# A fused attention and gated-FFN block: the fifth FFN product at two levels in both token passes, with two weight sums on Pool

## The chip, the cores and the metric

The kernel runs on one core of a Trainium2 chip. TensorE (PE) multiplies, with a weight load (PEld) ahead of each matmul; VectorE (DVE), ScalarE (ACT) and GpSimd (POOL) do the elementwise work; SyncE (SP) issues nearly all DMAs. Each engine runs its own instructions in program order, and semaphores order the engines against each other. The metric is device microseconds (us) of one execution.

## The reference

For 2048 tokens of width D = 1024: layer norm, linear attention, a residual, layer norm, a gated FFN of width F = 3584, a second residual.

```python
h = x + A(layernorm(x))          # qkv, phi, linear attention, @ wo
y = layernorm(h)
gate = y @ W_gate;  gate = gate * (gate > 0)
up   = y @ W_up
out  = h + (gate * up) @ W_down
```

## The kernel before, in words

**Order.** The program plans every instruction with its readers and writers (`PL.add`) and derives the semaphores; the order on each engine is the order of the calls. After attention come the output product `a4_mm` with its residual `a4_h` (L1252), then two token passes of 1024 tokens. Each pass is 14 FFN units (`ffn_unit`) and a down projection (`down_pass`).

**A unit.** A unit makes two 128-column blocks of gate (even unit) or of up (odd unit), called u = 0 and 1, for 1024 tokens. It does so with seven products instead of eight (Strassen's scheme in Winograd's form): `P1`, `P6`, `P2`, `P5`, `P7`, `P3`, `P4`, each of four 128x512 matmuls per u. The sums that this needs are the token sums `Ssum` (tile RC, four per pass) and the weight sums `Tring` (tile RO): four per unit, `T1` to `T4`, made by `t_sums` (L1354) from the weights in RWG, each a subtraction of 128x1024 elements for both u at once. `T2` reads `T1`, and `T4` reads `T2`. `T1` is the weight side of `P5`, `T2` of `P6`, `T3` of `P7`, `T4` of `P4`. All four run on DVE, apart from those of the very first unit, which run on Pool in halves of 128x512.

**Two levels.** In pass 1 (`L2F = (1,)`) product 5 is itself split into seven smaller ones, `M1` to `M7`, of 2 matmuls of 128x256 each, where the plain form has 8 matmuls of 128x512. This takes inner token sums `xs5` (`x_inner`, four per pass), inner weight sums `g5` (`w_inner`, three instructions per unit, L1395), copies of partial results on ACT (`M1c`, `M6c`, `M7c`, `M4c`), and two additions `s5_add` on DVE (L1514). The copies and additions use one PSUM bank with `M4` and `M3`: on PE, `M4` waits until `s5_add(1)` has read that bank.

**Evacuation.** The results of `P7` and `P3` get product 5 added on DVE (`evac5`, L1456, PSUM plus a tile). An even unit then applies relu on ACT; an odd unit multiplies gate and up on DVE (L1462, and L1470 straight from PSUM).

**Work between the products.** `fill` is a list of DVE work for the next unit, of which `fillin(n)` takes n items at fixed places of the unit; `mid` holds lists that are run at other fixed places. In pass 0 these bring in the weight sums for the down projection (`wd_sums` L706, `wl_sums` L729 on DVE and L745 on Pool, with their stores), sums of finished activations (`hh_sums`, L1366 and L1369), and the late layer norm of tokens 1024 to 2047 (ACT squares and means, small Pool steps, ACT norm). The Pool sums of `wl_sums` wait for the PE instruction just planned. At the end of a unit SP issues weight loads for a unit three later.

A pair of units in pass 0 (even, odd) is the period of this schedule.

Of the kernel before, what the change touches and what calls it, by code (L numbers as in the profile page):

```python
# [6 lines left out]
ALU = mybir.AluOpType  # L7
# [125 lines left out]
def bass_sequential_preLN__linear_attn_block__glu_gated_reglu__prompt_kernel(  # L133
# [15 lines left out]
    _, S, D = A_x.shape  # L149
# [7 lines left out]
    NW = 512  # L157
# [48 lines left out]
    with es:  # L206
# [70 lines left out]
        ftmp = RE[:, 0:(NO + NOT) * D].bitcast(f32).rearrange("p (a b) -> p a b", b=SBW)  # L277
        c22 = RE[:, 2 * D:3 * D].rearrange("p (a b) -> p a b", b=SBW)
        c12 = RE[:, 3 * D:4 * D].rearrange("p (a b) -> p a b", b=SBW)
        xs5 = RE[:, 4 * D:6 * D].bitcast(f16).rearrange("p (j k t) -> p j k t", j=4, k=2)  # L280
        g5 = RE[:, 6 * D:8 * D].bitcast(f16).rearrange("p (s j c) -> p s j c", s=2, j=4)
        hnE = RE[:, 4 * D:8 * D].rearrange("p (t a c) -> p t a c", t=STB, c=P)
        o0 = (NO + NOT) * D
        x2r = RE[:, o0:o0 + NX2 * D].rearrange("p (a b) -> p a b", a=NX2)
# [49 lines left out]

        hres = RX[:, 0:NHR * NW].rearrange("p (a b) -> p a b", a=NHR)
        outst = RX[:, 2 * NHR * NW:(2 * NHR + NOS) * NW].rearrange("p (a b) -> p a b", a=NOS)
        lsum = RX[:, 0:16 * HNW].bitcast(f16).rearrange("p (o j c) -> p o j c", o=4, j=4)
        dsf = RX[:, 0:STB * 2 * SBW].bitcast(f32).rearrange("p (a b) -> p a b", a=STB)
        zeros_t = hsb[:, 0, 0:512]
# [130 lines left out]
        def flat(x):  # L470
            return [b for row in x for b in (flat(row) if isinstance(row, list) else [row])]
# [38 lines left out]
            b_.over = B_E + B_bt + [B_TWq[2], B_junk]  # L510
        for b_ in B_hres + B_ds:
            b_.over = B_lsum
        for b_ in B_outst:
            b_.over = B_E + B_bt + [B_TWq[2], B_junk]
        for b_ in B_hnE:
            b_.over = B_o + B_oT
        for b_ in B_V:
            b_.over = B_hnE
        for b_ in flat(B_hh) + B_out2:
            b_.over = flat(B_xnT) + flat(B_pqT)  # L520
        for b_ in flat(B_pqT):
            b_.over = flat(B_wkv)
# [814 lines left out]
                lambda: add(3, blk(1, 0), Ssum[:, 1], ALU.subtract, [B_S[1]] + bl(0)),  # L1337
            ]

        def t_sums(L, eng="dve"):  # L1340
            i = L % NWG
            k = L % NTR
            n = 1 if eng == "pool" else 2

            def wb(kk, h, u):
                return wring[:, i + u:i + u + n, kk * KH:(kk + 1) * KH, h * P:(h + 1) * P]

            def tb(j, u):
                return Tring[:, k + u:k + u + n, j]

            def add(j, f0, f1, td):
                def go(u):
                    r = range(u, u + n)
                    PL.add(eng, lambda e: e.tensor_tensor(out=tb(j, u), in0=f0(u), in1=f1(u), op=ALU.subtract),  # L1354
                           reads=[B_w[i + x] for x in r] + ([B_T[k + x][td] for x in r] if td is not None else []),
                           writes=[B_T[k + x][j] for x in r], name="T%d_%d" % (j + 1, L))
                return [lambda u=u: go(u) for u in range(0, 2, n)]

            return (add(0, lambda u: wb(0, 1, u), lambda u: wb(0, 0, u), None) +
                    add(1, lambda u: wb(1, 1, u), lambda u: tb(0, u), 0) +  # L1360
                    add(2, lambda u: wb(1, 1, u), lambda u: wb(0, 1, u), None) +
                    add(3, lambda u: wb(1, 0, u), lambda u: tb(1, u), 1))
# [7 lines left out]
                                                    in1=hh[:, f1, SBW:2 * SBW], op=ALU.subtract),  # L1370
                   reads=[B_hh[f1][0]], writes=[B_hh[f1][1]], name="D3_%d" % q)

        def x_inner():
# [12 lines left out]
        def w_inner(n):  # L1386
            z = n % 2
            k = (2 * n) % NTR
            bt = [B_T[k][0], B_T[k + 1][0]]

            def T(kh, u):
                return Tring[:, k + u, 0, 2 * kh:2 * kh + 2, :].rearrange("p a c -> p (a c)")

            def add(dst, a_, b_, rd, wr):
                PL.add("dve", lambda e: e.tensor_tensor(out=dst, in0=a_, in1=b_, op=ALU.subtract), reads=bt + rd,  # L1395
                       writes=wr, name="g5_%d" % n)
# [10 lines left out]
        def ffn_unit(ps_, n, fill, mid):  # L1407
# [3 lines left out]
            kt = [(Lg + u) % NTR for u in range(2)]  # L1411
            f0 = 2 * (n - up)
            BA, BE, BB, BC_ = [0, 1], [2, 3], [4, 5], [6, 7]
            if ps_ in L2F:
                BE, BB = BB, BE
            if up:
                BB, BC_ = BC_, BB
# [65 lines left out]
            def p2(u):  # L1483
                prod(u, BA[u], w_blk(u, 1, 0), a_blk(1, 0), False, "P2")
                evac(0, 0, u, BA[u], "h11")

            if ps_ in L2F:
                cX, cD, c0 = ps[:, BE[1], 0:SHB], ps[:, BE[1], SHB:2 * SHB], ps[:, BE[0], 0:SHB]
                B_X = B_D = B_bank[BE[1]]
                tb = [B_T[kt[0]][0], B_T[kt[1]][0]]  # L1490
# [5 lines left out]

                def B_(kh, u):
                    return (lambda kk: Tring[:, kt[u], 0, 2 * kh + kk, :]), [tb[u]]

                def G(j):  # L1500
                    return (lambda kk: g5[:, z, j, kk * P:(kk + 1) * P]), [B_g5[z][j]]
# [24 lines left out]
                s5(1, 0, cX, B_X, "M6c")  # L1526
                sub(c0, B_bank[BE[0]], B_(1, 0), A(0, 1), False, "M2")
                fillin(2 if up else 3)
                p2(0)
                go(mid[2])  # L1530
                sub(cX, B_X, G(2), XS(2), False, "M7")
                s5(1, 1, cX, B_X, "M7c")
                s5_add(1)
                p6(0)
                p2(1)
                p6(1)
# [6 lines left out]
                       writes=[B_X, B_s5[0]], name="M4c")  # L1543
                go(later)
                later.clear()
                fillin(2 if up else 3)
                s5_add(0)
                B_s5[1].over = B_s5q[1]
# [523 lines left out]
        flush()  # L2072
        LAG = NOT
        pool_t = t_sums(0, "pool")
        for t in range(NE, NST + LAG + 1):
            if LAG <= t < NST + LAG:
                a4_mm(t - LAG)
            if t < NST:
                a2_num(t)
                a2_div(t)  # L2080
            if LAG <= t < NST + LAG:
                a4_h(t - LAG)
            if LAG + 1 <= t < TPP + LAG + 1:
                a4_norm(t - LAG - 1)
            if t in (5, 7, 18, 19):
                load_w_next()
            if t >= 9:
                run(pool_t, 1)
            if 15 <= t < 19:
                s_sums()[t - 15]()  # L2090
        load_w_next()
        load_w_next()
        for q in range(NWR):
            load_wraw(q)
        wl_q = []
        L2F = (1,)
        ln_q = []
        LQ = 3

        for p_ in range(NPASS):  # L2100
            fill = []
            for q in range(NPAIR):
                if q + 1 < NPAIR:
                    t_ = t_sums((p_ * NPAIR + q + 1) * 2)
                    if p_ in L2F:
                        t_ = t_[0:1] + w_inner(q + 1) + t_[1:]
                    fill = fill + t_
                mid = [[], [], [], [], []]
                if q > 0 and q % 2 == 0:
                    mid[0].append(lambda q=q: hh_sums(q - 2))  # L2110
                    mid[3].append(lambda q=q: hh_sums(q - 1))
                if p_ == 0:
# [8 lines left out]
                        ln_q.append(n_)  # L2121
                    if 2 <= q - LQ < 2 + STB:
                        early_t(q - LQ - 2)
                    mid[0] += wl_q
                    wl_q.clear()
                    if q % 2 == 0:
                        mid[1].append(lambda: wd_sums(q))
                    else:
                        w0_, w1_, mid[4] = wl_sums(q // 2)
                        mid[0].append(lambda: wd_sums(q))  # L2130
                        if q < NPAIR - 1:
                            mid[1].append(w0_)
                            wl_q.append(w1_)
                        else:
                            mid[0] = [load_wd_next] * 2 + mid[0] + [w0_, w1_]
                else:
                    if q == 0:
                        claim(B_xr + flat(B_lx), B_wd[0:NWS - 3])
# [24 lines left out]
            assert not fill  # L2163
            hh_sums(NPAIR - 2)
            hh_sums(NPAIR - 1)
            if p_ in L2F:
                claim(B_V, B_xs5 + flat(B_g5))
            late = []
            if p_ + 1 < NPASS:
# [13 lines left out]
                if p_ + 1 in L2F:  # L2183
                    def claim_xs():
                        claim(B_xs5, B_V)
                        claim(flat(B_g5), B_V)

                    gi = w_inner(0)
                    xi = x_inner()
# [62 lines left out]
```

## Time and profile before

| | us |
|---|---|
| median of 3 runs | 725.68 (725.53 to 727.32) |
| the profiled execution, its own time | 725.28 |
| its span | 723.5 |
| pass 0, 14 units | 229.75 to 398.96 |
| down projection of pass 0 | 398.96 to 476.76 |
| pass 1, 14 units | 476.76 to 643.20 |
| down projection of pass 1 | 643.20 to the end |

| stretch | length | PE busy | DVE busy | ACT busy | POOL busy |
|---|---|---|---|---|---|
| pass 0, units | 169.21 | 169.21 | 144.38 | 109.32 | 40.14 |
| pass 1, units | 166.44 | 166.44 | 134.10 | 83.53 | 3.54 |

Busy time is the time in which at least one instruction of the engine is in flight; back-to-back instructions overlap by some tens of ns, so that busy time is less than count times mean. A row of a timeline gives start, duration, engine, source line, operation, tiles (out<-in), shapes and count, and in brackets the idle time before it with what ended it. The source line of a helper is shared by all its callers: L767 is every matmul, L772 every plain ACT copy, L1661 the down projection's additions.

### The profile page before, as it was taken

What the parts mean: (1) busy time and instruction counts of PE and PEld (TensorE: products, weight loads), DVE (VectorE), ACT (ScalarE), POOL (GpSimd) and SP (SyncE); (2) the same over time, 40 slices, a digit from 0 to 9 for tenths busy, and PEclk for the clock granted to TensorE, in tenths of its full rate; (3) what the DMA queues carried; (4) which work ended last, traced back from release to release, by engine and by line L of the source; (5) the groups of instructions that cost most, each with busy time, mean ns of one, the idle gap of its engine ahead of it and who ended that gap; (6) DMA issues with size and microseconds to landing.
All of it is one profiled execution on the core that took longest, in us unless ns stands there. A gap on an engine that the chain in (4) does not pass through costs nothing.

```text
span 723.5 us, 12104 instructions
## 1 busy us (share of the span) xinstructions
PE 717.1 (99%) x4521; PEld 384.6 (53%) x4521; DVE 587.2 (81%) x1024; ACT 361.0 (50%) x632; POOL 109.5 (15%) x177
## 2 busy tenths in 40 slices
PE   9999999999999999999999999999999999999998
PEld 4444444344444444444444568865555555547887
DVE  7878867799776889888988787787889877887984
ACT  4878666764841456687757111035455545423010
POOL 1411100000360103322321002310000000000331
PEclk9999999999999999999999999999999999999999
DMA  9652244023998897999999999994555572037996
GB/s 316 207 115 61 37 131 156 13 29 68 195 229 258 245 267 228 281 296 264 326 298 276 302 265 315 320 211 119 149 166 140 158 248 81 1 102 252 315 321 174
DMA packets 192986, 143.59 MB, mean 198 GB/s; under 512 B 51872, under 2 KB 170400, under 8 KB 192928
## 3 DMA queue, kind: packets, MB, share of 16 engines
q1 hardware_dynamic: 188224, 138.50, 66.6%
q0 software_dynamic: 4032, 3.67, 3.6%
q8 instruction: 35, 0.57, 0.3%
q10 hardware_dynamic: 672, 0.66, 0.3%
q14 instruction: 23, 0.19, 0.1%
HBM read 98.76 MB, written 32.51 MB: 181 GB/s over the span
## 4 chain that ended last, share of the span: by engine, by line
PE 89%; DVE 6%; ACT 2%; issue 1%; SPq 1%; DMA 1%; POOL 0%; DVEq 0%; ACTq 0%
PE ps L767 89%; SPq L565 1%; DVE RAB L853 1%; DMA RE<-in_A_x_dram 1%; DVE RE L1228 1%; DVE RX L850 1%; ACT RX L846 1%; DVE RX L1069 1%; ACT RXH L805 1%; DVE RW L963 0%; DVE RWG L988 0%; ACT ps L772 0%; DVE RE L853 0%; DVE rden L1226 0%; DVE RE L1661 0%
## 5 line engine op out<-in xcount | busy, mean ns | idle before, releaser
L772 ACT ACTIVATE ps<-ps 128x512 f32<-128x512 f32 (+1 forms) x192 | 108.8, 567 | 218.0 <-PE ps L767 210.8
L767 PE MATMUL ps<-RC,RO 128*128 128x512 f16 x616 | 143.0, 369 | 0.0
L767 PE MATMUL ps<-RH,RWG 128*128 128x512 bf16 x448 | 108.1, 379 | 0.0
L767 PEld LDWEIGHTS ps<-RC,RO 128*128 128x128 f16 x616 | 60.3, 98 | 63.5
L767 PE MATMUL ps<-RC,RWG 128*128 128x512 f16 x320 | 76.8, 380 | 0.1
L767 PEld LDWEIGHTS ps<-RH,RWG 128*128 128x128 bf16 x448 | 43.8, 98 | 46.9
L767 PE MATMUL ps<-RH,RO 128*128 128x512 bf16 (+1 forms) x256 | 61.2, 379 | 0.0
L1470 DVE TENSOR_TENSOR RAB<-ps,RAB 128x512 bf16<-128x512 f32 x56 | 37.3, 686 | 29.4 <-PE ps L767 29.3
L767 PE MATMUL ps<-RW,RE 128*128 128x512 bf16 x256 | 57.6, 380 | 0.7 <-DVE RXH L1252 0.7
L1670 POOL DMA_DIRECT2D out_dram<-RX x20 | 17.9, 1256 | 263.3 <-DVE RX L1661 221.0
L767 PE MATMUL ps<-RAB 128*128 128x512 bf16 (+2 forms) x270 | 57.1, 351 | 0.1
L767 PE MATMUL ps<-RW,RAB 128*128 128x256 f16 (+3 forms) x362 | 52.9, 301 | 0.0
L767 PEld LDWEIGHTS ps<-RC,RWG 128*128 128x128 bf16 (+1 forms) x320 | 30.0, 98 | 40.0 <-ACT ps L772 6.0
L772 ACT ACTIVATE RE<-ps 128x512 f32<-128x512 f32 (+1 forms) x64 | 31.5, 503 | 37.8 <-PE ps L767 37.8
L767 PEld LDWEIGHTS ps<-RW,RAB 128*128 128x128 f16 (+1 forms) x362 | 35.4, 98 | 14.4 <-DVE RX L1661 0.2
L1354 DVE TENSOR_TENSOR RO<-RWG 128x1024 f16<-128x1024 bf16 x54 | 37.0, 684 | 6.4 <-DMA RWG<-in_B_W_up_dram 4.7
L1661 DVE TENSOR_TENSOR RE<-ps,RE 128x512 f32<-128x512 f32 x44 | 30.2, 687 | 14.3 <-PE ps L767 13.8
L772 ACT ACTIVATE RAB<-ps 128x512 bf16<-128x512 f32 x56 | 33.3, 594 | 16.6 <-PE ps L767 16.3
L767 PEld LDWEIGHTS ps<-RH,RO 128*128 128x128 f16 (+1 forms) x256 | 24.4, 98 | 30.0 <-ACT RX L772 1.6
L1456 DVE TENSOR_TENSOR RAB<-ps,RE 128x512 bf16<-128x512 f32 x56 | 37.1, 685 | 2.8 <-PE ps L767 1.9
L767 PEld LDWEIGHTS ps<-RW,RE 128*128 128x128 bf16 x256 | 24.0, 98 | 28.7 <-DVE RXH L1252 1.2
L1465 ACT ACTIVATE RAB<-RAB 128x1024 bf16<-128x1024 bf16 x28 | 29.5, 1055 | 19.4 <-DVE RAB L1456 18.9
(163 smaller groups left out, 1168.7 us busy)
## 6 DMA issues: line engine op xcount, KB each, us to landing
RWG<-in_B_W_gate_dram SPq DMA_DIRECT2D x28, 512.0 KB, 6.8
RWG<-in_B_W_up_dram SPq DMA_DIRECT2D x28, 512.0 KB, 5.5
RW<-l_scr SPq DMA_DIRECT2D x20, 448.0 KB, 5.8
RW<-in_B_W_down_dram SPq DMA_DIRECT2D x14, 512.0 KB, 5.7
t_scr<-RW SPq DMA_DIRECT2D x14, 512.0 KB, 5.0
l_scr<-RX SPq DMA_DIRECT2D x7, 1024.0 KB, 5.9
RE<-l_scr SPq DMA_DIRECT2D x15, 448.0 KB, 4.5
RE<-in_A_x_dram SPq DMA_DIRECT2D x23, 256.0 KB, 3.3
```

The lines of the kernel that those rows point to most:

```text
L565: return PL.add(eng, lambda e: e.dma_start(dst_ap, src_ap), reads=reads, writes=writes, slot=slot, name=name)
L767: lambda e: e.matmul(out_ap, lhsT, rhs, start=start, stop=stop, skip_group_check=skip),
L772: PL.add("act", lambda e: e.activation(out=dst, in_=src, func=func), reads=reads, writes=writes, name=name)
L805: PL.add("act", lambda e: e.activation(out=junk[:, c0:c1], in_=src[:, c0:c1], func=func, scale=scale, accum_out=sv[:, col:col + 1]), reads ...
L846: PL.add("act", lambda e: e.activation(out=Et[:, k, :], in_=src, func=ACTF.Exp), reads=[src_buf], writes=[B_E[k]], name=name + "_exp")
L850: PL.add("dve", lambda e: e.tensor_scalar(out=Et[:, k, :], in0=Et[:, k, :], scalar1=1.0, scalar2=1e-6, op0=ALU.min, op1=ALU.add), reads=[] ...
L1354: PL.add(eng, lambda e: e.tensor_tensor(out=tb(j, u), in0=f0(u), in1=f1(u), op=ALU.subtract), reads=[B_w[i + x] for x in r] + ([B_T[k + x] ...
L1456: PL.add("dve", lambda e: e.tensor_tensor(out=d, in0=src, in1=ftmp[:, u, :], op=ALU.add), reads=[bsrc, B_s5[u]], writes=[db], name=name)
L1465: PL.add("act", lambda e: e.activation(out=d, in_=d, func=ACTF.Relu), reads=[], writes=db, name=name)
L1470: PL.add("dve", lambda e: e.tensor_tensor(out=d, in0=bank(b), in1=d, op=ALU.mult), reads=[B_bank[b]], writes=[db], name=name)
L1661: PL.add(eng, lambda e: e.tensor_tensor(out=dst, in0=in0, in1=in1, op=op), reads=reads, writes=writes, name=name)
L1670: PL.add("pool", lambda e: e.dma_start(dst, src, accum_op=ALU.add), reads=[bsrc], writes=[B_hscr[st]], slot=sl, name="acc_%d_%d" % (st, dh))
```

## The change

- Product 5 goes at two levels in pass 0 too, apart from its first unit: `L2F = (0, 1)` and the condition `ps_ + n > 0`. The inner sums of pass 0 have their own places (`xs5s[0]` in RX, `g5s[0]` in RAB); the token ones are made at the end of attention (steps 16 and 17 of that loop), with `w_inner(0, 0)` at its last steps.
- In both passes `T3` and `T4` of the next unit go to Pool (`tail="pool"`), still 128x1024 each.
- The places of other work shift: in a two-level unit `mid[2]` runs after `M4c` and not before `M7`, `wl_sums`' second half runs in `mid[3]`, and the last unit of pass 0 spreads its `mid[0]` over `mid[5]`, `mid[6]` and `mid[0]`.

```diff
-        def t_sums(L, eng="dve"):
+        def t_sums(L, eng="dve", tail=None):
...
             def add(j, f0, f1, td):
+                en = tail if tail and j >= 2 else eng
+
                 def go(u):
                     r = range(u, u + n)
-                    PL.add(eng, lambda e: e.tensor_tensor(out=tb(j, u), in0=f0(u), in1=f1(u), op=ALU.subtract),
+                    PL.add(en, lambda e: e.tensor_tensor(out=tb(j, u), in0=f0(u), in1=f1(u), op=ALU.subtract),
...
-            if ps_ in L2F:
+            if ps_ == 1:
                 BE, BB = BB, BE
...
-            if ps_ in L2F:
+            if ps_ in L2F and ps_ + n > 0:
...
                 fillin(2 if up else 3)
+                go(mid[5])
                 p2(0)
-                go(mid[2])
                 sub(cX, B_X, G(2), XS(2), False, "M7")
                 s5(1, 1, cX, B_X, "M7c")
                 s5_add(1)
+                go(mid[6])
                 p6(0)
...
                 go(later)
                 later.clear()
+                go(mid[2])
                 fillin(2 if up else 3)
                 s5_add(0)
...
         pool_t = t_sums(0, "pool")
+        gi = w_inner(0, 0)
...
+            if t == 16:
+                for f_ in x_inner(0)[0:2]:
+                    f_()
+            if t == 17:
+                for f_ in x_inner(0)[2:4]:
+                    f_()
+            if t >= NST:
+                run(gi, 1)
...
-        L2F = (1,)
+        L2F = (0, 1)
...
-                    t_ = t_sums((p_ * NPAIR + q + 1) * 2)
+                    t_ = t_sums((p_ * NPAIR + q + 1) * 2, tail="pool")
                     if p_ in L2F:
-                        t_ = t_[0:1] + w_inner(q + 1) + t_[1:]
+                        t_ = t_[0:1] + w_inner(p_, q + 1) + t_[1:]
...
-                    mid[0] += wl_q
+                    mid[3] += wl_q
...
-                            mid[0] = [load_wd_next] * 2 + mid[0] + [w0_, w1_]
+                            mid[5] = [load_wd_next] * 2 + mid[0]
+                            mid[6], mid[0] = [w0_], [w1_]
```

More of the change, by code (lines that the diff above doesn't have):

```diff
@@ L279, in bass_sequential_preLN__linear_attn_block__glu_gated_reglu__prompt_kernel @@
         c12 = RE[:, 3 * D:4 * D].rearrange("p (a b) -> p a b", b=SBW)
-        xs5 = RE[:, 4 * D:6 * D].bitcast(f16).rearrange("p (j k t) -> p j k t", j=4, k=2)
-        g5 = RE[:, 6 * D:8 * D].bitcast(f16).rearrange("p (s j c) -> p s j c", s=2, j=4)
+        o5 = NFT * TOK
+        g5s = [x.bitcast(f16).rearrange("p (s j c) -> p s j c", s=2, j=4)
+               for x in (RAB[:, o5:o5 + 2 * D], RE[:, 6 * D:8 * D])]
         hnE = RE[:, 4 * D:8 * D].rearrange("p (t a c) -> p t a c", t=STB, c=P)
@@ L336, in bass_sequential_preLN__linear_attn_block__glu_gated_reglu__prompt_kernel @@
         outst = RX[:, 2 * NHR * NW:(2 * NHR + NOS) * NW].rearrange("p (a b) -> p a b", a=NOS)
+        xs5s = [x.bitcast(f16).rearrange("p (j k t) -> p j k t", j=4, k=2)
+                for x in (RX[:, 2 * NHR * NW:(2 * NHR + NOS) * NW], RE[:, 4 * D:6 * D])]
         lsum = RX[:, 0:16 * HNW].bitcast(f16).rearrange("p (o j c) -> p o j c", o=4, j=4)
@@ L512, in bass_sequential_preLN__linear_attn_block__glu_gated_reglu__prompt_kernel @@
             b_.over = B_lsum
-        for b_ in B_outst:
+        for b_ in B_xs5:
             b_.over = B_E + B_bt + [B_TWq[2], B_junk]
@@ L518, in bass_sequential_preLN__linear_attn_block__glu_gated_reglu__prompt_kernel @@
             b_.over = B_hnE
-        for b_ in flat(B_hh) + B_out2:
+        for b_ in flat(B_hh) + flat(B_g5):
             b_.over = flat(B_xnT) + flat(B_pqT)
@@ L1371, in hh_sums, with x_inner @@
                    reads=[B_hh[f1][0]], writes=[B_hh[f1][1]], name="D3_%d" % q)
-        def x_inner():
+        def x_inner(ps_):
+            xs5 = xs5s[ps_]
             def A(t, k):
@@ L1384, in x_inner, with w_inner @@
                     lambda: add(2, A(0, 0), A(1, 0), ALU.subtract), lambda: add(3, A(0, 1), X(1), ALU.subtract)]
-        def w_inner(n):
+        def w_inner(ps_, n):
+            g5 = g5s[ps_]
             z = n % 2
@@ L1498, in B_ @@
                     return (lambda kk: Tring[:, kt[u], 0, 2 * kh + kk, :]), [tb[u]]
+                g5, xs5 = g5s[ps_], xs5s[ps_]
                 def G(j):
@@ L2103, in bass_sequential_preLN__linear_attn_block__glu_gated_reglu__prompt_kernel @@
                 if q + 1 < NPAIR:
-                    t_ = t_sums((p_ * NPAIR + q + 1) * 2)
+                    t_ = t_sums((p_ * NPAIR + q + 1) * 2, tail="pool")
                     if p_ in L2F:
-                        t_ = t_[0:1] + w_inner(q + 1) + t_[1:]
+                        t_ = t_[0:1] + w_inner(p_, q + 1) + t_[1:]
                     fill = fill + t_
-                mid = [[], [], [], [], []]
+                mid = [[], [], [], [], [], [], []]
                 if q > 0 and q % 2 == 0:
@@ L2165, in bass_sequential_preLN__linear_attn_block__glu_gated_reglu__prompt_kernel @@
             hh_sums(NPAIR - 1)
-            if p_ in L2F:
+            if p_ == 0:
+                claim(B_outst, B_xs5)
+                claim(B_out2, flat(B_g5))
+            else:
                 claim(B_V, B_xs5 + flat(B_g5))
@@ L2186, in claim_xs @@
                         claim(flat(B_g5), B_V)
-                    gi = w_inner(0)
-                    xi = x_inner()
+                    gi = w_inner(1, 0)
+                    xi = x_inner(1)
                     late += [(claim_xs, (6, 0)), (xi[0], (6, 3)), (xi[1], (6, 4)), (xi[2], (6, 4)), (xi[3], (6, 5))]
```

## The prediction

> **What bounds the kernel now.** I read the page's head first, then the chain that ended last in order of time, then a table of busy time with one stretch per FFN unit.
>
> ```profile
> PE 717.1 (99%) x4521; PEld 384.6 (53%) x4521; DVE 587.2 (81%) x1024; ACT 361.0 (50%) x632; POOL 109.5 (15%) x177
> ```
> ```profile
> 177.21 505.76 PE ps L767 x3106
> ```
> ```profile
> core 0: us, PE busy (x) PEld busy (x) DVE busy (x) ACT busy (x) POOL busy (x), PEclk, DMA share, GB/s
> ...
> 278.10:290.19 12.09, 12.09 (x58) 5.47 (x57) 11.95 (x21) 9.23 (x15) 2.34 (x4) 1.00 0.84 240
> 290.19:302.27 12.08, 12.08 (x58) 5.47 (x56) 9.71 (x19) 8.51 (x14) 5.17 (x10) 1.00 1.14 316
> ...
> 500.54:512.43 11.89, 11.89 (x64) 6.07 (x63) 10.90 (x25) 6.61 (x12) 0.00 (x0) 1.00 0.55 154
> 512.43:524.32 11.89, 11.89 (x64) 6.05 (x63) 9.64 (x21) 5.32 (x10) 0.00 (x0) 1.00 0.56 156
> ```
>
> From 177 to 683 us the chain is PE alone, without a gap, so both passes run at the speed of their matmuls. The table shows what stands behind it. The first two rows are one pair of pass 0 (plain product 5): 24.17 us of PE, and DVE busy 11.95 + 9.71 = 21.66. The last two are one pair of pass 1 (two levels): 23.78 us, DVE 20.54. DVE has 2.5 us per pair left in pass 0, and it is the next limit.
>
> **The gain on PE.** A plain unit takes 12.09 us, a two-level one 11.89, both from stretches without a PE gap. 13 units of pass 0 change (the first stays plain): 13 x 0.20 = 2.6 us less, 722.7 if nothing else moves. The rest asks whether DVE can follow.
>
> **DVE's own work per pair in pass 0.**
>
> ```profile
> L1354 DVE TENSOR_TENSOR RO<-RWG 128x1024 f16<-128x1024 bf16 x54 | 37.0, 684 | 6.4 <-DMA RWG<-in_B_W_up_dram 4.7 <-DMA RWG<-in_B_W_gate_dram 1.8
> L1514 DVE TENSOR_TENSOR RE<-ps,RE 128x256 f32<-128x256 f32 x28 | 11.9, 425 | 12.2 <-ACT RE L1541 8.6 <-ACT RE L772 3.6
> L1395 DVE TENSOR_TENSOR RE<-RO,RE 128x256 f16<-128x256 f16 x28 | 8.1, 290 | 0.7
> L1395 DVE TENSOR_TENSOR RE<-RO 128x512 f16<-128x512 f16 x14 | 5.9, 422 | 0.2
> L1354 POOL TENSOR_TENSOR RO<-RWG 128x512 f16<-128x512 bf16 x4 | 4.6, 1152 | 0.0
> ```
>
> T3 and T4 leave: four instructions, 0.61 us each (the distance of starts in a run of them), -2.4. The inner weight sums come: 2 x (0.42 + 2 x 0.29) = +2.0. The two additions per unit come: 4 x 0.43 = +1.7. That is 21.66 - 2.4 + 2.0 + 1.7 = 22.9 of 23.78 us. Alone it fits, with 0.9 us per pair to spare. In pass 1 only the sums leave: 20.54 - 2.4 = 18.1.
>
> **Pool's price for a weight sum.** No row has one of 128x1024. At 128x512 it took 1.152 us (above); a Pool subtraction of 128x256 undisturbed took 0.67 (below). The step of 0.48 per 256 columns gives 2.1 us. Doubling the larger gives 2.3, the upper end; below the line through both rows nothing points. I take 2.1; 0.2 more would cost at most 4 x 0.2 x 6 pairs = 4.8 us. Four per pair are 8.4 us on an engine that is busy 7.5 (2.34 + 5.17): Pool is not the limit. T4 waits on Pool for DVE's T2, and behind it stand L745 and the late norm's small steps, which nobody needs within the unit.
>
> The Trainium skill, page GPSIMD Engine Reference, section Engine selection, puts a two-input elementwise operation on GpSimd at about twice VectorE's time. By that page a sum would take an estimated 1.4 us, the delay below would be about 1.3 per unit, and the end about 733. This case's rows disagree: three times DVE's pace.
>
> **What Pool's sums do to DVE.** This is where the change is decided. Times in these rows are start and duration.
>
> ```profile
> 252.83 0.67 POOL L745 TENSOR_TENSOR RAB<-RW,RAB 128x256 f16<-128x256 bf16 x1
> ```
> ```profile
> 301.97 2.21 POOL L745 TENSOR_TENSOR RAB<-RW,RAB 128x256 f16<-128x256 bf16 x2
> ```
> ```profile
> 301.88 0.69 DVE L1462 TENSOR_TENSOR RAB<-RAB,RE 128x1024 bf16<-128x1024 bf16 x1
> 302.49 2.23 DVE L729 TENSOR_TENSOR RX<-RW 128x1024 f16<-128x1024 f16 x2
> 304.65 0.68 DVE L1470 TENSOR_TENSOR RAB<-ps,RAB 128x512 bf16<-128x512 f32 x1
> ```
> ```profile
> 350.83 1.29 DVE L729 TENSOR_TENSOR RX<-RW 128x1024 f16<-128x1024 f16 x2
> ```
> ```profile
> 681.27 1.08 DVE L1601 TENSOR_TENSOR RWG<-RAB 128x1792 f16<-128x1792 bf16 x1
> 681.44 3.04 POOL L1661 TENSOR_TENSOR RE<-RE,RX 128x512 f32<-128x512 f32 x2 [0.91 <-DVE RE L1661]
> ...
> 683.60 1.83 DVE L1601 TENSOR_TENSOR RWG<-RAB 128x1792 f16<-128x1792 bf16 x1
> ```
>
> Two L729 sums take 1.29 us with Pool idle and 2.23 beside two Pool subtractions, which themselves grew from 1.34 to 2.21. The order fits a strict turn: Pool waits for the DVE instruction that runs, then DVE waits for Pool's whole instruction. At 683.60 DVE's sum took 1.83 instead of 1.08, until Pool was through. All these DVE instructions read two SBUF tiles. One that reads PSUM and one tile kept its 0.68 beside Pool (the L1456 rows around 250 us). So a Pool sum holds off DVE's next two-tile instruction, and all behind it, for up to 2.0 us (2.1 less some 0.1 of start). In pass 0 about three fifths of DVE's time is two-tile work: weight sums, inner sums, L706, L729, L1366, L1369, L1462.
>
> Where do the four meet? T4 waits for T2, the last DVE item before the two evacuations of `P3` (PSUM, 1.28 us as a run). It starts under them and holds the instruction behind them for 2.0 - 1.3 = 0.7. T3, queued on Pool before or behind it, then gets its turn after one DVE instruction and meets two-tile work (L706 in even units, L1462 or L729 in odd ones): 2.0. That is 2.7 per unit, 5.4 per pair. Ends: each sum finds such a run, 4 x 0.7 = 2.8; none does, 4 x 2.0 = 8.0. I take 5.4, since the order of the program gives just one such run behind T2.
>
> **Sum.** DVE needs 22.9 + 5.4 = 28.3 us per pair against 24.17 before: 4.1 more, for the six pairs of units 2 to 13: 24.6. PE meets it at `M4`, which waits for `s5_add(1)`; in the pass-1 unit that starts at 500.54 that addition ended at 505.52 and `M4` started at 506.81, so DVE can be 1.3 us late once without cost. Unit 1 gains 0.2. In pass 1 DVE needs 18.1 + 5.4 = 23.5 of 23.78: it just fits, 0. So 725.3 + 24.6 - 1.5 = 748.4, from the profiled run's own 725.28 (span 723.5 and 1.8 around it, 0.4 under the median of the runs): 748 us.
>
> **Parts that I cost at nothing.** The token sums (4 x 0.42) and `w_inner(0, 0)` (1.0), 2.7 us of DVE at 220 to 231: DVE then waits 4.65 us for weights until 235.88, and the residual add that frees the bank pair of the last output product ended at 224.79, 1.5 before it was needed; without that cover up to 1.2 us. ACT's copies: 1.72 against 1.20 per unit (0.37 + 2 x 0.38 + 0.59 against 2 x 0.60), under 9.23 of 12.09 busy; if ACT were late too, the copies before `M7` would hold PE. DMAs: the store of L729's sums and the late norm's store and reload move later in their unit, past the stores of L706 on SP. The last store was issued at 391.94 and the loads that follow it from 404.11, so 12 us cover a shift of 4. Weight loads behind them on SP are three units ahead. Pool's small norm steps queue among its sums; ACT's norm waits for them, and its result is used a pass later.
>
> **Rivals.**
> - *The sums find cover (faster, 722.7).* Holds if Pool delays DVE by less than 0.9 us per pair, 0.2 per sum: then DVE keeps 23.78. For it: 40% of DVE's time in pass 0 and its waits for PE (1.95 and 0.17 us in the odd unit) don't contend. Against: those waits are already spent in the 22.9, and no instruction is tied to a PSUM run as the L745 ones are.
> - *Mostly covered (728 to 740).* The lower end of the delay, 2.8 per pair: 25.7 - 24.17 = 1.5, times 6, less 1.5: 733. It needs DVE to be at `P7`, `P3` or gate evacuations whenever Pool starts.
> - *More than DVE's delay (760 to 775).* No cover: 30.9 - 24.17 = 6.7, times 6, less 1.5: 764; pass 1 then needs 26.1 of 23.78 too, some 8 more. PE also may slow down once it idles: at the start, after idling, 12 matmuls took 5.30 us, 0.44 each against 0.22 later.
>
> ```profile
> 1.37 5.30 PE L767 MATMUL ps<-RXH 128*128 128x512 bf16 x12 [1.37 <-POOL RXH L546]
> ```
>
> The Trainium skill, page TensorE: Matmul & The Clock Gate, section HAM oscillation, warns of PE gaps over about 3.4 us, after which PE runs at half rate. By that page one such gap per pair would cost an estimated 1.7 us each, 10 in all. No row before shows such a gap in mid-kernel.
> - *The change does less than it says.* The first unit's three `g5` sums have no reader, and 13 of 14 units change; the matmul count settles it, within the 0.2 us of a unit.
>
> **How the numbers follow.** Forecast (740 to 760): 0.62. Mostly covered: 0.13. Beyond: 0.10. Faster: 0.12. Within 0.3% (2.2 us, about what a measurement of this kernel tells from no change): 0.03. The last two lie below 728 and half of "beyond" above 765, 0.20 together, so the range is 728 to 765; the forecast's own is 740 to 760. Slower: 0.62 + 0.13 + 0.10 = 0.85.
>
> **What would show it.** Right: PE gaps in most units of pass 0 after unit 1, ended by L1514; L1354 on Pool at 2.1 us or more; L706, L729, L1462 or L1366 longer than before by up to 2 us where Pool runs; DVE busy near all of pass 0; pass-1 units at 11.89. Wrong: units of 11.89 in pass 0, which would mean that Pool's sums run under PSUM work or that DVE keeps its turn; gaps ended by ACT or a DMA; or gaps mainly in pass 1.

## The result and the profile after

The changed kernel takes 763.85 us (median of 4 runs, 762.60 to 764.87) against 725.63 before (median of 4 runs, too): a ratio of 1.052, 95% interval 1.0498 to 1.0542, 38.2 us slower. The forecast was 748, range 728 to 765: slower, as forecast, but by 38 and not by 22. The time lies only 1 us inside the stated range, and 4 us above the 740 to 760 that the forecast gave as its own. The profiled execution took 764.2 (span 762.5), 38.9 over the one of before.

The page's head, and the shares of the chain that ended last, of the changed kernel:

```profile
PE 728.4 (96%) x4599; PEld 392.1 (51%) x4599; DVE 650.8 (85%) x1044; ACT 364.4 (48%) x658; POOL 224.8 (29%) x229
PE 44%; DVE 17%; issue 2%; DMA 1%; SPq 0%; DVEq 0%
```

There are 78 more matmuls, 13 units of 6, so the change does what it says. The chain that ended last could be followed back only to 262.67 us here, so that its shares, 44% PE and 17% DVE, can't be set beside the 89% and 6% of before, which cover the whole span. In pass 0 it runs through DVE: of the 30.65 us from the end of one stall at 293.56 to the end of a later one at 324.21, 24.23 are DVE's and 3.68 PE's.

Busy time by stretch: one pair of pass 0 between two stalls, one unit of pass 1, a long piece of pass 1.

```profile
core 0: us, PE busy (x) PEld busy (x) DVE busy (x) ACT busy (x) POOL busy (x), PEclk, DMA share, GB/s
324.21:354.81 30.60, 25.99 (x124) 12.30 (x124) 29.11 (x45) 18.46 (x32) 15.94 (x16) 0.94 0.92 244
515.34:527.23 11.89, 11.79 (x63) 5.89 (x61) 10.83 (x17) 6.51 (x12) 9.89 (x7) 1.00 0.79 177
550.00:690.00 140.00, 140.00 (x726) 70.62 (x725) 127.38 (x208) 66.00 (x122) 47.95 (x21) 1.00 0.46 131
```

This pair of pass 0 takes 30.60 us instead of 24.17. The units of pass 0 run from 230.56 to 437.13, 206.57 us instead of 169.21: 37.4 more. Another 0.8 arises ahead of them, and 0.4 in the down projection behind them. Pass 1 now starts at 515.34 and before at 476.76, 38.6 later, and its units keep 11.89. So nearly all of the loss lies in the units of pass 0. The pairs are not all alike: the first stall, in unit 2, is 3.47 us long, and units 1, 3 and 13 have none at `M4`.

PE's waits (in total, times, longest), and PE's timeline in an even unit:

```profile
PE ps L770 <- DVE RE L1524: 22.7, 10, 3.5
```
```profile
324.21 0.39 PE L770 MATMUL ps<-RC,RAB 128*128 128x256 f16 x2 [2.43 <-DVE RE L1524]
324.44 0.38 PE L770 MATMUL ps<-RX,RO 128*128 128x256 f16 x2
324.66 3.15 PE L770 MATMUL ps<-RC,RO 128*128 128x512 f16 x8
327.60 2.36 PE L770 MATMUL ps<-RC,RWG 128*128 128x512 f16 x8
```

PE stands at `M4` for `s5_add(1)` (L1514 before, L1524 now): 2.4 us in an even unit of these rows, some 1.8 in an odd one. The eight matmuls of `P7` behind the long stall then take 3.15 us and those of `P3` 2.36, where 1.89 is usual. Here is Pool in the same pair, and then DVE:

```profile
327.71 0.30 POOL L823 TENSOR_SCALAR s<-s 128x1 f32<-128x1 f32 x1 [4.44 <-ACT RE L808]
330.88 0.50 POOL L826 TENSOR_TENSOR s<-s 128x1 f32<-128x1 f32 x1 [2.87 <-ACT RE L808]
...
332.35 2.12 POOL L1359 TENSOR_TENSOR RO<-RWG 128x1024 f16<-128x1024 bf16 x1
334.42 2.30 POOL L1359 TENSOR_TENSOR RO<-RWG,RO 128x1024 f16<-128x1024 bf16 x1
...
348.78 2.57 POOL L1359 TENSOR_TENSOR RO<-RWG 128x1024 f16<-128x1024 bf16 x1
351.31 2.56 POOL L1359 TENSOR_TENSOR RO<-RWG,RO 128x1024 f16<-128x1024 bf16 x1
```
```profile
327.91 0.69 DVE L1464 TENSOR_TENSOR RAB<-ps,RE 128x512 bf16<-128x512 f32 x1 [1.04 <-PE ps L770]
...
331.25 1.28 DVE L1464 TENSOR_TENSOR RAB<-ps,RE 128x512 bf16<-128x512 f32 x2
332.44 5.36 DVE L709 TENSOR_TENSOR RW<-RW 128x512 f16<-128x512 bf16 x4
...
340.31 1.54 DVE L709 TENSOR_TENSOR RW<-RW 128x512 f16<-128x512 bf16 x4
341.78 1.43 DVE L1403 TENSOR_TENSOR RAB<-RO,RAB 128x256 f16<-128x256 f16 x2
...
348.22 3.68 DVE L732 TENSOR_TENSOR RX<-RW 128x1024 f16<-128x1024 f16 x2
351.82 1.28 DVE L1478 TENSOR_TENSOR RAB<-ps,RAB 128x512 bf16<-128x512 f32 x2
353.02 1.41 DVE L1359 TENSOR_TENSOR RO<-RWG 128x1024 f16<-128x1024 bf16 x1
```

Four L709 sums take 1.54 us with Pool idle, and 5.36 beside the two Pool sums of the even unit. Two L732 take 3.68 instead of 1.29, `T1` 1.41 instead of 0.69. The rows that read PSUM (L1464, L1478) keep their 1.28, also at 351.82 in the middle of a Pool sum. Per pair that is 3.8 + 2.4 + 0.7 = 6.9 us of DVE held off, put down to the weight sums here; L748's subtractions hold off 1.0 more (L1403 1.43 for 0.62, one L1470 0.92 for 0.69). The split is not sharp: with all sums on DVE (below) L748 alone stretches that L732 row by some 0.5. The total of 7.9 stands. At 327.91 DVE waits 1.04 for the slow `P7`. What is left of the pair, 30.60 - 7.9 - 1.0 = 21.7, is DVE's own work, with some 0.5 of small gaps in it (DVE is busy for 29.11).

PE's slow stretch is one of the clock. Three successive stretches of 3.41 us, the clock being the third number from the end:

```profile
321.72:325.13 3.41, 0.98 (x8) 0.64 (x8) 3.38 (x7) 1.85 (x4) 1.55 (x1) 1.00 1.03 322
325.13:328.54 3.41, 3.41 (x10) 1.22 (x9) 2.30 (x7) 2.49 (x4) 0.30 (x1) 0.50 1.54 249
328.54:331.95 3.41, 3.41 (x19) 1.73 (x18) 3.34 (x8) 2.92 (x5) 0.99 (x2) 1.00 0.64 213
```

After a stretch in which PE was busy for 0.98 of 3.41 us, the granted clock is 0.50 for the next 3.41. This comes once per pair, after the stall in the even unit; the records show it at six places in pass 0. The shortest of these stalls, before 293.56, is 1.98 us:

```profile
291.00:294.41 3.41, 1.43 (x9) 0.69 (x8) 3.38 (x7) 1.78 (x4) 1.62 (x1) 1.00 1.01 342
294.41:297.83 3.42, 3.42 (x9) 1.22 (x8) 2.27 (x6) 2.56 (x4) 0.30 (x1) 0.50 1.04 272
```

### The profile page after: what moved, and what is told of

The parts are those of the page before. It is cut to its first block, busy times and chain, and to the rows that moved or that the text cites. A ratio compares the mean times of both kernels' runs of the same rounds, so it can differ in the third digit from the quotient of the medians.

```text
span 762.5 us, 12427 instructions
## 1 busy us (share of the span) xinstructions
PE 728.4 (96%) x4599; PEld 392.1 (51%) x4599; DVE 650.8 (85%) x1044; ACT 364.4 (48%) x658; POOL 224.8 (29%) x229
## 3 DMA queue, kind: packets, MB, share of 16 engines
q0 software_dynamic: 4032, 3.67, 3.3%
## 4 chain that ended last, share of the span: by engine, by line
PE 44%; DVE 17%; issue 2%; DMA 1%; SPq 0%; DVEq 0%
PE ps L770 44%; DVE RW L709 4%; DVE RX L732 3%; DVE RO L1359 2%; DVE RAB L1478 2%; DVE RE L1464 2%; DVE RAB L1464 1%; DVE RAB L1470 1%; DMA r_scr<-RW 1%; DVE RE L1524 1%; DMA RW<-in_B_W_down_dram 1%; DVE RE L1403 1%; DVE RAB L1403 0%; DVE RX L1673 0%; DVE RAB L1374 0%
## 5 line engine op out<-in xcount | busy, mean ns | idle before, releaser
L775 ACT ACTIVATE ps<-ps 128x512 f32<-128x512 f32 (+1 forms) x205 | 113.9, 555 | 232.1 <-PE ps L770 211.8
L770 PE MATMUL ps<-RC,RO 128*128 128x512 f16 (+1 forms) x564 | 140.6, 376 | 0.0
L770 PE MATMUL ps<-RH,RWG 128*128 128x512 bf16 x448 | 110.2, 379 | 0.5 <-ACT ps L775 0.5
L1359 POOL TENSOR_TENSOR RO<-RWG,RO 128x1024 f16<-128x1024 bf16 (+1 forms) x30 | 62.7, 2092 | 118.8 <-issue 72.6
L770 PEld LDWEIGHTS ps<-RC,RO 128*128 128x128 f16 x564 | 56.8, 101 | 53.2 <-issue 6.7
L770 PE MATMUL ps<-RC,RWG 128*128 128x512 f16 x320 | 79.9, 390 | 0.6 <-ACT ps L775 0.5
L1359 POOL TENSOR_TENSOR RO<-RWG 128x1024 f16<-128x1024 bf16 (+1 forms) x30 | 68.5, 2286 | 23.1 <-DMA RWG<-in_B_W_up_dram 22.6
L823 POOL TENSOR_SCALAR s<-s 128x1 f32<-128x1 f32 x23 | 9.1, 396 | 126.9 <-ACT RX L808 101.4
L1478 DVE TENSOR_TENSOR RAB<-ps,RAB 128x512 bf16<-128x512 f32 x56 | 37.1, 681 | 10.6 <-PE ps L770 10.6
L1464 DVE TENSOR_TENSOR RAB<-ps,RE 128x512 bf16<-128x512 f32 x56 | 36.8, 684 | 7.4 <-PE ps L770 7.1
L775 ACT ACTIVATE RE<-ps 128x256 f32<-128x256 f32 (+1 forms) x64 | 25.8, 415 | 35.1 <-PE ps L770 35.1
```

What stands on the lines that cost most here:

```text
L770: lambda e: e.matmul(out_ap, lhsT, rhs, start=start, stop=stop, skip_group_check=skip),
L775: PL.add("act", lambda e: e.activation(out=dst, in_=src, func=func), reads=reads, writes=writes, name=name)
L823: PL.add("pool", lambda e: e.tensor_scalar(out=sv[:, 2:3], in0=sv[:, 0:1], scalar1=sv[:, 0:1], scalar2=EPS, op0=ALU.mult, op1=ALU.subtract ...
L1359: PL.add(en, lambda e: e.tensor_tensor(out=tb(j, u), in0=f0(u), in1=f1(u), op=ALU.subtract), reads=[B_w[i + x] for x in r] + ([B_T[k + x][ ...
L1464: PL.add("dve", lambda e: e.tensor_tensor(out=d, in0=src, in1=ftmp[:, u, :], op=ALU.add), reads=[bsrc, B_s5[u]], writes=[db], name=name)
L1478: PL.add("dve", lambda e: e.tensor_tensor(out=d, in0=bank(b), in1=d, op=ALU.mult), reads=[B_bank[b]], writes=[db], name=name)
```

## Experiments

All ratios are against the kernel before, with 95% intervals. The theory: Pool's weight sums and DVE's two-tile sums take turns at SBUF, and DVE, held off, makes PE late at `M4`. Rivals: Pool delivers `T3` and `T4` too late; the added work at two levels or the moved places are too much for DVE alone; the clock.

| kernel | us | ratio |
|---|---|---|
| changed kernel | 763.85 | 1.052 [1.0498, 1.0542] |
| two levels, all sums on DVE | 732.59 | 1.0097 [1.0081, 1.0114] |
| Pool sums alone, pass 0 plain | 735.92 | 1.0138 [1.0123, 1.0153] |
| T3 and T4 left out | 723.91 | 0.9973 [0.9962, 0.9983] |
| T3 and T4 as Pool memsets | 723.93 | 0.9975 [0.9966, 0.9985] |
| `T3` on Pool under PSUM work, `T4` on DVE | 723.83 | 0.9975 [0.9965, 0.9984] |
| two levels in even units only | 725.19 | 0.9992 [0.9983, 1.0000] |
| added matmuls in the stalls | 756.78 | 1.0424 [1.0408, 1.0440] |
| late-norm steps at unit's end | 761.47 | 1.0490 [1.0475, 1.0504] |
| late-norm steps at unit's end, added matmuls in even units | 750.82 | 1.0343 [1.0325, 1.0360] |

### Each half alone

```diff
-                    t_ = t_sums((p_ * NPAIR + q + 1) * 2, tail="pool")
+                    t_ = t_sums((p_ * NPAIR + q + 1) * 2)
```

> The changed kernel with T3 and T4 back on DVE; two levels in pass 0 and all moved places stay. Theory (Pool's weight sums hold DVE off): in the changed kernel's pair of pass 0 from 324 to 355 us DVE was busy 29.1 us, of which some 7 us are rows stretched beside Pool; so DVE's own work is about 22, and with the two sums of each unit back (4 x 0.61) about 24.4 per pair, against 24.17 before and 23.78 of PE. Time 723 to 729. Rival 1 (the two-level product's own DVE and ACT work is too much): DVE gets more work than in the changed kernel, so 760 or more. Rival 2 (the moved places of the other work are at fault): 750 to 765.

Measured 732.59: slower than before, and 3.6 us above the upper end of what was expected. Stretch of one pair, and two rows of DVE's timeline:

```profile
310.97:336.38 25.41, 23.85 (x123) 11.88 (x125) 24.96 (x49) 18.28 (x32) 6.80 (x12) 1.00 1.10 299
```
```profile
305.82 1.76 DVE L732 TENSOR_TENSOR RX<-RW 128x1024 f16<-128x1024 f16 x2
...
324.78 1.44 DVE L1403 TENSOR_TENSOR RAB<-RO,RAB 128x256 f16<-128x256 f16 x2
```

DVE is saturated: 24.96 busy of 25.41, with 1.5 us stretched by the subtractions that L748 always had on Pool (0.47 and 0.82 here, 0.23 on an L1470). Two levels, with the moved places, cost 1.6 us per pair over PE's 23.78. Without those 1.5 us it would about fit; that is worked out, not run.

The other half, on the kernel before:

```diff
-                    t_ = t_sums((p_ * NPAIR + q + 1) * 2)
+                    t_ = t_sums((p_ * NPAIR + q + 1) * 2, tail="pool")
```

> The kernel before with T3 and T4 of each unit on Pool in both passes, and nothing else of the change. Theory: DVE 21.7 - 2.4 = 19.3 us per pair of pass 0, plus some 5 to 7 held off, 24 to 26 against 24.17 of PE: 726 to 742, and L706, L729 or L1462 rows stretched. Rivals 1 and 2: DVE is relieved and nothing else changes, 725.6.

Measured 735.92, 10.1 us slower, though DVE has less work than before. PE's waits, and a DVE instruction with the Pool sum that it met:

```profile
PE ps L767 <- DVE RE L1458: 6.6, 5, 1.5
PE ps L767 <- DVE RAB L1458: 4.0, 5, 1.1
```
```profile
312.73 2.23 DVE L1371 TENSOR_TENSOR RAB<-RAB 128x512 f16<-128x512 bf16 x1
```
```profile
312.50 2.18 POOL L1356 TENSOR_TENSOR RO<-RWG,RO 128x1024 f16<-128x1024 bf16 x1 [4.49 <-DVE RO L1356]
```

A sum of 0.42 us took 2.23. So Pool's sums cost time even without two levels. The halves cost 6.7 and 10.1 us against the runs of before that were taken with them, and together they cost 38.2. That fits a spare time of DVE that each of them uses up alone, so that the second finds none; some 7 us of the difference are the clock (below).

### Is it the lateness of the sums or their reading?

The two sums left out; `P7` then reads `T1` and `P4` reads `T2`, so the output is not the reference's.

```diff
-                prod(u, BB[u], t_blk(u, 2), s_blk(2), False, "P7")
+                prod(u, BB[u], t_blk(u, 0), s_blk(2), False, "P7")
...
-                prod(u, BB[u], t_blk(u, 3), a_blk(1, 1), False, "P4")
+                prod(u, BB[u], t_blk(u, 1), a_blk(1, 1), False, "P4")
...
+                    t_[2:] = [lambda: None] * 2
```

> The changed kernel without T3 and T4: P7 reads T1 and P4 reads T2 in their place, so these two sums of every unit are left out of the computation and PE does the same number of matmuls. Theory: nothing holds DVE off any more and its own 22 us fit in 23.78, so the matmuls' gain shows: 722.7 (722 to 724). Rival 1: the additions and inner sums stay, 750 or more. Rival 2: the places stay, 750 or more.

723.91, no stalls. And each sum as two Pool memsets of the same tile, with the same waits:

```diff
+                    if en != eng:
+                        for m in range(2):
+                            PL.add(en, lambda e: e.memset(tb(j, u), 0.0),
...
+                        return
```

> The changed kernel with each of T3 and T4 on Pool replaced by two memsets of 128x1024 on Pool into the same tile, with the same waits and readers; the values of these sums are left out. Pool is about as busy as before (a memset of 128x512 took 0.53 us) but reads no SBUF. Theory in its narrow form (Pool's reads hold off DVE's second SBUF input): 722 to 726. Rival 3 (PE or DVE waits because T3 and T4 come late from Pool's queue, or a busy Pool is enough): 750 or more. Between 730 and 750: writes hold DVE off too, in part.

723.93. Pool and DVE in an even unit of this kernel:

```profile
314.96 3.86 POOL L1361 MEMSET RO<- 128x1024 f16 x4
```
```profile
315.07 1.54 DVE L709 TENSOR_TENSOR RW<-RW 128x512 f16<-128x512 bf16 x4
```

Pool is busy for 3.86 us per unit, almost as long as with the sums (4.4), and at the same places of its queue, but the four L709 beside it take 1.54 and not 5.36. Everything else of the change is still there: the added inner sums and additions, the moved places, the waits for Pool. So the 40 us between this kernel and the changed one come from what Pool's sums do beside keeping their place in the queue and writing, which is to read SBUF; they do not come from a late Pool. That Pool reads two tiles and not one is not tried separately.

### `T3` under cover

Pass 1 as before; in pass 0 `T4` on DVE, `T3` on Pool in halves, each tied to the PE and DVE instructions planned last, at places where DVE goes on to read PSUM. L748's subtractions get the same tie, and the late norm's Pool steps go to the unit's end.

```diff
+        def t3_halves(L):
+            i, k = L % NWG, L % NTR
+
+            def go(u):
+                PL.add("pool", lambda e: e.tensor_tensor(out=Tring[:, k + u:k + u + 1, 2],
...
+                       deps=tie(), reads=[B_w[i + u]], writes=[B_T[k + u][2]], name="T3_%d" % L)
+            return [lambda u=u: go(u) for u in range(2)]
+
+        def tie():
+            return [PL.prog["pe"][-1], PL.prog["dve"][-1]]
...
+            t3_at = ("h11", "P4") if up else ("P7", "P3")
...
-                       deps=[PL.prog["pe"][-1]], reads=x[1] + y[1], writes=[B_lsw[z][j]], name="WM%d_%d" % (j, m))
+                       deps=tie(), reads=x[1] + y[1], writes=[B_lsw[z][j]], name="WM%d_%d" % (j, m))
...
-                    t_ = t_sums((p_ * NPAIR + q + 1) * 2, tail="pool")
+                    t_ = t_sums((p_ * NPAIR + q + 1) * 2)
+                    if p_ == 0:
+                        t3 = t3_halves((p_ * NPAIR + q + 1) * 2)
+                        t_ = t_[0:2] + t_[3:4]
```

> Pass 1 as in the kernel before (all four weight sums on DVE). In pass 0, with two levels, T4 goes back to DVE, T3 stays on Pool in two halves of 128x512 (1.15 us each on Pool), and each half waits for the PE and DVE instructions planned just ahead of it, so that it starts under DVE work that reads PSUM (the evacuations of P7 and P3 in even units, the runs around P2 and P4 in odd ones). The Pool sums of L745 and L748 are tied in the same way, and the late norm's small Pool steps move to the end of their unit. Theory (Pool's read of SBUF holds off only DVE instructions that read two SBUF tiles, so cover removes the price): DVE's own work 23.9 per pair as with all sums on DVE, less 1.2 for the two T3, some 22.7, plus under 1 of hold-off, against 23.78 of PE: 722.5 to 726, faster than before by up to 0.4%. Rival (DVE is held off whatever its operands are, or the ties make Pool late and DVE waits for Pool): four halves a pair at 1.15 each beside the 1.5 that L748 costs already put DVE at 26 to 28 us a pair, 735 to 748.

723.83: faster than both kernels, by 0.25% than the one before. PE's matmuls alone allow 722.7 from the profiled execution of before, or 723.1 from the median. One pair, then Pool, then DVE:

```profile
307.90:331.68 23.78, 23.78 (x125) 12.14 (x124) 22.93 (x48) 18.11 (x32) 12.03 (x17) 1.00 1.10 302
```
```profile
313.92 1.15 POOL L1383 TENSOR_TENSOR RO<-RWG 128x512 f16<-128x512 bf16 x1 [2.88 <-DVE RO L1369]
...
318.32 1.15 POOL L1383 TENSOR_TENSOR RO<-RWG 128x512 f16<-128x512 bf16 x1 [0.50 <-PE ps L770]
```
```profile
313.67 1.28 DVE L1494 TENSOR_TENSOR RAB<-ps,RE 128x512 bf16<-128x512 f32 x2
314.86 1.62 DVE L709 TENSOR_TENSOR RW<-RW 128x512 f16<-128x512 bf16 x4
```

The four halves of the pair lie almost wholly under rows that read PSUM, and the L709 run behind the one at 313.92 keeps 1.62. PE has no gap in the pair. This run changes several things at once; what it shows is that such Pool sums can be had without making PE wait, not which tie was worth what, nor that both sums would fit.

### Half of the two-level work

Two levels in even units of pass 0 only, all sums on DVE.

```diff
+        def two(p, n):
+            return p == 1 or n > 0 and n % 2 == 0
...
-            if ps_ in L2F and ps_ + n > 0:
+            if two(ps_, n):
...
-                    t_ = t_sums((p_ * NPAIR + q + 1) * 2, tail="pool")
-                    if p_ in L2F:
+                    t_ = t_sums((p_ * NPAIR + q + 1) * 2)
+                    if two(p_, q + 1):
...
-                            mid[5] = [load_wd_next] * 2 + mid[0]
-                            mid[6], mid[0] = [w0_], [w1_]
+                            mid[0] = [load_wd_next] * 2 + mid[0] + [w0_, w1_]
```

> Two levels in pass 0 only in even units from unit 2 on; odd units keep the plain product 5; all four weight sums on DVE in both passes, so Pool's load is as before. Theory (DVE's room decides and half of the added work fits): DVE's own work per pair 21.66 + 1.0 + 0.85 = 23.5 against 12.09 + 11.89 = 23.98 of PE, so six pairs gain up to 0.2 each: 724 to 726.5 with short gaps at most. Rival (DVE is late even so, since what L748 on Pool holds off, some 1.5 per pair, comes on top: 25.0 against 23.98): six pairs at +0.8 over before, some 730, near the time of two levels in all units with all sums on DVE (732.6).

725.19: inside the theory's range, which also holds the time of before, and 5 us under the rival's. PE runs without a gap in the units, but the 0.5 us gained are hardly more than the measurement resolves. Beside the 732.59 with two levels in all units, this fits DVE's room, and not the form of the product, as what decides.

### What the stalls cost through the clock

The changed kernel with 16 more matmuls ahead of `M4`, results unread:

```diff
+                if ps_ == 0 and n > 1:
+                    for kk in range(16):
+                        mm(ps[:, BE[0], SHB:2 * SHB], hnT[:, kk % KH, 0:P], Ssum[:, 0, kk % KH, 0:SHB], True, True,
+                           B_hnT[0:1] + [B_S[0]], B_bank[BE[0]], "filler", skip=True)
                 sub(cX, B_X, G(3), A(1, 1), False, "M4")
```

> The changed kernel with 16 more matmuls of 128x256 ahead of M4 in units 2 to 13 of pass 0, whose results nobody reads: 16 x 0.11 = 1.77 us of PE work per unit, put where PE stalls for 1.8 to 2.4 us. Theory A (the stalls also cost clock: the half-rate windows of 3.41 us, one a pair, make matmuls up to 1.3 us late, DVE waits 1.0 for PE, and both are lost): PE is busy in the stalls, the windows of half rate are gone, and each of six pairs is 0.5 to 1.7 us shorter in spite of the added matmuls: 754 to 761. Theory B (DVE alone sets the pair's length and the half-rate windows only eat PE's own slack): 764 as for the changed kernel, or up to 768 where the added matmuls stand in the way.

756.78: 192 matmuls more, and 7.1 us less than the changed kernel. A pair, and the two held-off runs of DVE:

```profile
324.01:353.46 29.45, 27.79 (x158) 15.00 (x156) 29.00 (x45) 18.18 (x33) 15.93 (x16) 1.00 0.92 250
```
```profile
329.46 5.35 DVE L709 TENSOR_TENSOR RW<-RW 128x512 f16<-128x512 bf16 x4
...
345.22 3.68 DVE L732 TENSOR_TENSOR RX<-RW 128x1024 f16<-128x1024 f16 x2
```

What Pool does to DVE is unchanged to 0.01 us. The half-rate windows and DVE's wait of 1.04 for `P7` are gone, and the pair is 1.15 shorter. So by this run the clock's share of the 38 us is some 7.

### What stood ahead of the sums in Pool's queue

The late norm's small Pool steps, which held `T3` and `T4` until 332.35 in the rows above, go to the end of their unit (`lnn` is the last of them):

```diff
-                PL.add("pool", lambda e: e.tensor_scalar(out=s2[:, k, 4:5], in0=s2[:, k, 0:1], scalar1=s2[:, k, 2:3],
+                late.append(lnn)
+
+            def lnn():
+                PL.add("pool", lambda e: e.tensor_scalar(out=s2[:, k, 4:5], in0=s2[:, k, 0:1], scalar1=s2[:, k, 2:3],
...
-            return m_, sq, norm
+            return m_, sq, norm, lambda: run(late, 9)
...
+            go(mid[7])
...
-                        m_, sq_, n_ = late_steps(q - LQ)
+                        m_, sq_, n_, lt_ = late_steps(q - LQ)
+                        mid[7].append(lt_)
```

> The changed kernel with one thing moved: the late norm's small Pool steps, which wait for an ACT square and stand ahead of T3 and T4 in Pool's queue, go to the end of their unit. Theory (in units with a late-norm step they make both Pool sums late, so that these miss the evacuations of P3 and hit the four L709 sums, which took 5.36 us instead of 1.55): T4 starts at T2's end under those evacuations, the L709 run is held off by one Pool sum at most (3.6 us or less), the even unit's gap at M4 shrinks from 2.4 by some 1 us or more, and six pairs give 4 to 10 us: 754 to 760. Rival (the sums meet two-tile work wherever they start, so the delay moves but stays): 762 to 766.

761.47: a miss on both, only 2.4 us. DVE, Pool, and the clock in successive stretches (L1369 is here what L1359 was):

```profile
334.59 2.56 DVE L709 TENSOR_TENSOR RW<-RW 128x512 f16<-128x512 bf16 x4
...
348.00 5.13 DVE L732 TENSOR_TENSOR RX<-RW 128x1024 f16<-128x1024 f16 x2
```
```profile
333.62 2.12 POOL L1369 TENSOR_TENSOR RO<-RWG,RO 128x1024 f16<-128x1024 bf16 x1 [9.05 <-DVE RO L1369]
...
347.50 2.56 POOL L1369 TENSOR_TENSOR RO<-RWG 128x1024 f16<-128x1024 bf16 x1
350.03 2.56 POOL L1369 TENSOR_TENSOR RO<-RWG,RO 128x1024 f16<-128x1024 bf16 x1
352.55 2.56 POOL L1369 TENSOR_TENSOR RO<-RWG 128x1024 f16<-128x1024 bf16 x1
```
```profile
321.25:324.66 3.41, 0.59 (x3) 0.10 (x1) 3.41 (x4) 1.43 (x3) 3.32 (x2) 1.00 1.07 334
324.66:328.07 3.41, 2.56 (x9) 1.21 (x10) 2.87 (x8) 1.64 (x3) 0.00 (x0) 0.50 1.08 198
328.07:331.49 3.42, 3.42 (x10) 1.22 (x9) 2.08 (x5) 1.97 (x4) 0.00 (x0) 0.50 0.47 153
```

The even unit does what was expected: `T4` starts at 333.62 under `P3`'s evacuation, and L709 takes 2.56 instead of 5.36. But three sums now follow each other in the odd unit, and L732 grows from 3.68 to 5.13. Added up over the pair, the hold-off falls from 7.9 to some 6.4 us. And the two stalls of a pair have become one of 3.67 us, after which the clock is here at 0.50 for two windows: DVE's waits for PE grow from 1.04 to 2.27. To see whether the clock ate the gain, both edits together, with 28 added matmuls in even units:

```diff
+                if ps_ == 0 and n > 1 and not up:
+                    for kk in range(28):
```

> The changed kernel with both of two single edits: the late norm's small Pool steps at the end of their unit, and added matmuls of 128x256 whose results nobody reads, here 28 of them (3.1 us) ahead of M4 in the even units from unit 2 on of pass 0, which is where PE stalls for 3.67 us once the late steps are moved. Moving alone gave only 2.4 us (761.5) and its DVE waited 2.3 us a pair for a PE at half rate, twice what it waited in the changed kernel. Theory (the moved steps do take some 1.5 us of hold-off from each pair, but the longer single gap gives it back through the clock): with PE kept busy the pair is DVE's 30.55 less 2.27 of waits for PE, 28.3, so six pairs save 13.8 on the changed kernel: 749 to 752, no half-rate windows. Rival (the two edits save the same thing, or the hold-off only moves): 755 to 757, the time with the added matmuls alone.

750.82, inside 749 to 752, with no half-rate window.

```profile
320.10:348.12 28.02, 27.18 (x152) 14.69 (x152) 27.57 (x46) 18.08 (x32) 16.67 (x16) 1.00 0.98 270
```
```profile
327.65 2.57 DVE L709 TENSOR_TENSOR RW<-RW 128x512 f16<-128x512 bf16 x4
...
340.53 5.14 DVE L732 TENSOR_TENSOR RX<-RW 128x1024 f16<-128x1024 f16 x2
```

Moving the steps alone gave 2.4 us, 16 added matmuls in every unit 7.1, and moving the steps with 28 in the even units 13.0. With the late steps out of the way and the clock kept up, the pair takes 28.02 us; 28.3 was expected of this run.

## Why the prediction was right, and where it was too small

- *Direction, mechanism and place: right.* PE stalls at `M4` behind L1524 in ten of the twelve units from unit 2 on; Pool's sums hold off two-tile work and leave the PSUM rows alone. The rows of L729 beside L745 in the trace of before told it, and the memset run confirms that it is Pool's reading.
- *Pool's price of 2.1 us: right for a sum that DVE does not hold up,* 2.12. The means of the sums of 128x1024 are 2.46 for `T3` and 2.24 for `T4`, up to 2.57 in the rows above, and so in part over the prediction's upper end of 2.3: the turns lengthen Pool's sums too. The Trainium skill, GPSIMD Engine Reference, section Engine selection, has about twice VectorE's time; 2.12 against 0.69 is three times. (With the prediction's estimate of 1.4 for a sum, its own terms give 732 and not the 733 that it names.)
- *DVE's own work of 22.9 per pair: 1.2 too high.* It measures 21.7. The 21.66 of before held 0.9 of hold-off already (L729 at 2.23 instead of 1.29), and the added instructions were priced by duration, where the distance of starts (0.34 for an L1524) counts.
- *Hold-off of 5.4 per pair: the term that was mis-sized.* It measures some 6.9 by the weight sums, 7.9 with L748. The step that failed is that `T4` starts under `P3`'s evacuations. In even units both sums stood behind the late norm's steps, which wait for ACT, and met the L709 run: 3.8 us there instead of 2.7. Those steps were named as work that waits behind the sums; that they also stand ahead of them was missed. With them moved the hold-off still is 6.4, since three sums then follow each other in the odd unit. That the pair of the last run, 28.02, comes near the forecast's 28.3 is luck: less own work and more hold-off than forecast cancel.
- *Clock: named as a rival, not in the sum.* It is 1.15 us per pair, 7 in all. The prediction's estimate of 1.7 per event, 10 in all, is half of about 3.4 us at half rate. The Trainium skill, TensorE: Matmul & The Clock Gate, section HAM oscillation, has about 1.67 us of throttled time per gap in its own kernel and counts half of that as lost, by which it would be an estimated 0.8 per event and 5 in all. Its condition, an idle gap over about 3.4 us, was not needed here: a gap of 1.98 sufficed.
- *The sum.* Own work -1.2, hold-off +2.5, waits for PE +1.0: 28.3 becomes 30.6, times six 13.8 of the 15.8 us that the profiled execution has over the forecast. Counted whole, the units of pass 0 took 37.4 us more where 23.1 were forecast, which is 14.3 over it; the other 1.5 lie outside them. No run separates the pairs that differ from the one shown.
- *The rival without cover comes to 764, the measured time, but not by what happened.* It has 22.9 + 8.0 us per pair where 21.7, 7.9 (L748 included) and 1.0 of waits were measured, and it expects a pass 1 that is late as well.
- *Pass 1 at no cost: right*, 11.89 per unit, though with its two Pool sums per unit DVE is busy for 127.38 of 140 us.
- *Parts at nothing: right within 1 us.* Without the two sums, or with memsets in their place, the kernel reaches 723.9 against 722.7 by PE's gain alone, or 723.1 from the median of the runs.

## What to carry to other kernels

Moving elementwise work from a nearly full DVE to an idle Pool is no relief where instructions of both that read two SBUF tiles meet: here 2.4 us per pair of DVE's work went away and some 6.9 us of being held off came. Look at what DVE does at the moment when Pool's instruction starts, and tie that start to DVE work that reads PSUM; also look at what stands ahead of it in Pool's queue. And once a stall of PE is forecast, price the clock behind it as well.

## What the runs showed of the hardware that was not expected

- Half the clock comes in windows of 3.41 us. In pass 0 of the changed kernel it went by how long PE was busy in such a window: full-clock windows with 0.49 to 1.43 us of PE were followed by one at 0.50, those with 2.22 or more were not. So a stall of 1.98 within one window was enough, and one of 1.90 across two (2.59 and 2.34 us of PE) was not. With the late steps moved, a stall of 3.81 us lay across windows with 2.06 and 0.95 us of PE, and only the second was followed by half rate.
- Pool writing (memsets, 3.86 us at a time) leaves DVE's two-tile sums at their pace; Pool reading two tiles stretched them to three and a half times (1.54 to 5.36).
- PE work that nobody needs, placed in a stall, made the kernel 7.1 us faster.
